# Transposing the row of maxima one group later in an attention and feed-forward kernel, with other groups for the middle tile's maxima and six buffers for the sums of p

## The chip, the cores and the metric

The kernel runs on one core of a Trainium2 chip. The metric is the device time of one execution in microseconds (us); several executions are timed, and the median counts. The engines have separate instruction streams and wait for each other through semaphores: PE multiplies matrices (its weight loads are listed apart as PEld), DVE, ACT and POOL do elementwise work and reductions, and SP issues the transfers.

## The reference

Attention for 8 batches of 8 heads, 1152 positions of width 64, in which the queries are averaged in pairs (576 rows are left), and then a feed-forward layer over the 4608 rows:

```
q_pool = q.reshape(B, H, S // 2, 2, D).mean(axis=3)
scores = (1 / sqrt(D)) * (q_pool @ k^T)
attn   = exp(scores - max over keys);  attn /= (sum over keys + 1e-9)
x      = attn @ v                      # 4608 x 512 after regrouping
h      = x @ w_in                      # 512 -> 2048
out    = (h - tanh(h)) @ w_out         # 2048 -> 512
```

## The kernel before, in words

**Two stages.** The attention stage goes through 32 pairs of heads; the feed-forward stage follows and uses the attention's output from device memory. Numbers are split in a high and a low part (`hi`, `lo`), so that each product is three matmuls.

**A clock of units.** The attention stage is ordered by hand. A pair has 36 units. Every sixth unit begins a group of three key tiles for one half of the queries, so a pair has six groups, which begin at its units 0, 6, 12, 18, 24 and 30. On each even unit `scores` (L271) issues eight matmuls into a `ps_s` tile: `hi` by `hi`, `hi` by `lo`, `lo` by `hi`, and last `ones_k` by `mb`, which subtracts the row's maximum. ACT then takes the exponential into the group's tile `p_f`. When a group is through, POOL adds its three key tiles' exponentials (`z_part`, L288, two additions into a tile `z`); 11 units after the group's begin `pv` (L294) multiplies `p_f` by v into `ps_o`. Once for each half of the queries, one group after that half's last `pv`, at units 11 and 29, `z_sums` (L314) multiplies its three `z` tiles by ones, into the single tile `ps_z`; until then those tiles are held. Each engine's queue holds its instructions in the order in which this loop issues them.

**Maxima.** The maxima of a pair must be known before its first scores. So, during the pair ahead of it, `max_part` (L224) multiplies `hi` by `hi` for three thirds of the keys and for five tiles of queries: tiles 0 to 3 into a `ps_s` tile, two in each group; the middle tile, 4, into `ps_z`. DVE reduces each into `mx` a unit later. `ps_s` has three buffers and is shared by scores and maxima; `ps_z` has one buffer, shared by the middle tile's maxima, the sums and the transposition.

**The row of maxima.** `max_rows` (L240) runs 23 units ahead of the pair (`row`, L436): on DVE two reductions into `nm`, then the two instructions that write `m2` (shown as `m` in the profile): a copy that rounds and a subtraction. Then, as many units after `row` as `steps` says, `turn` transposes `m2` on PE into `ps_z`, with ACT's copy to `mt` a unit later (`out`), `there` sends `mt` to `m_dram`, and `back` fetches it as two rows into `mb`. On SP's queue `back` waits until `there` has landed.

**What the change touches.** The pool `zp` that holds the tiles `z` (L147), `steps` (L436) and the list `mids` of the middle tile's three units (L438, and L451 for the third pair). The second pair's own `row, steps` (L449) and the first's (L443) stand apart: in the first pair everything is packed closer, and the maxima of the second and the third pair are taken there and in the second pair.

The order of the feed-forward stage is left to a scheduler.

Of the kernel before, what the change touches and what calls it, by code (L numbers as in the profile page):

```python
# [43 lines left out]
def kernel(  # L44
# [97 lines left out]
    with ExitStack() as actx:  # L142
# [1 line left out]
        sm = actx.enter_context(tc.tile_pool(name="sm", bufs=2))  # L144
        op = actx.enter_context(tc.tile_pool(name="op", bufs=1))
        pf = actx.enter_context(tc.tile_pool(name="pf", bufs=4))
        zp = actx.enter_context(tc.tile_pool(name="zp", bufs=4))  # L147
        vp = actx.enter_context(tc.tile_pool(name="vp", bufs=2))
        hl = actx.enter_context(tc.tile_pool(name="hl", bufs=3))
        ld = actx.enter_context(tc.tile_pool(name="ld", bufs=2))  # L150
# [29 lines left out]
        def add(u, f, *args, at=at):  # L180
            at.setdefault(u, []).append(lambda: f(*args))
# [251 lines left out]
        for pi in range(n_pair):  # L433
            u = pi * U
            units = dict(load=-92, query_sums=-80, hi_q=-70, hi_k=-68, hi_k2=-66, lo_q=-64, lo_k=-52, lo_k2=-46, load_v=-40)
            row, steps = -23, (4, 6, 12)  # L436
            spots = [x for g in range(6) for x in ((at, -60 + G * g + 5), (early, -60 + G * g + 6))]
            mids = [-49, -37, -31]  # L438
            if pi == 0:
                units.update(load=-60, query_sums=-52, hi_q=-51, hi_k=-50, hi_k2=-49, lo_q=-22, lo_k=-21, lo_k2=-20)  # L440
                spots = [(at, -48 + 2 * i) for i in range(12)]
                mids = [-43, -35, -27]
                row, steps = -24, (2, 3, 4)  # L443
            if pi < 3:
                v0 = -U * pi
                if pi == 1:
                    units.update(load=v0 - 58, query_sums=v0 - 25, hi_q=v0 - 20, hi_k=v0 - 19, hi_k2=v0 - 18, lo_q=-28, lo_k=-16, lo_k2=-10)
                    mids = [v0 + 5, v0 + 11, v0 + 17]
                    row, steps = v0 + 25, (2, 3, 6)  # L449
                if pi == 2:  # L450
                    mids = [v0 + 29, v0 + 35, v0 + 41]  # L451
                if pi > 0:
                    spots = [x for g in range(4) for x in ((early, v0 + 24 * (pi - 1) + G * g), (at, v0 + 24 * (pi - 1) + G * g + 2),
                                                           (at, v0 + 24 * (pi - 1) + G * g + 5))]
            add(u + units["load"], load, pi)
            add(u + units["query_sums"], query_sums, pi, dve if pi < 1 else pool)
            for what, f in (("hi", hi_part), ("lo", lo_part)):
                add(u + units[what + "_q"], f, pi, 0, SQ)
                add(u + units[what + "_k"], f, pi, SQ, 2 * SQ)
                add(u + units[what + "_k2"], f, pi, 2 * SQ, KQ)  # L460
            add(u + units["hi_k2"], middle, pi)
            for i, (when, x) in enumerate(spots):
                add(u + x, max_part, u + x, pi, *divmod(i, 3), at=when)
            for c, x in enumerate(mids):
                add(u + x, max_part, u + x, pi, 4, c)
            add(u + units["load_v"], load_v, pi)
            add(u + row, max_rows, u + row, pi, steps)
# [162 lines left out]
```

## Time and profile before

| | |
|---|---|
| median of 3 runs | 1810.62 us (1803.29 to 1811.96) |
| profiled execution, own time | 1805.21 us |
| its span | 1803.4 us |
| attention stage, about | 0 to 979 us of the span |
| one steady pair (480.00 to 509.21 us) | 29.21 us |
| PE, DVE, ACT, POOL busy in the span | 95%, 81%, 58%, 58% |
| mean granted TensorE clock | 0.991 |

In the profile's rows, an instruction is named by its engine, its line and by what it writes and reads (`mx<-ps_s`). Nearly all of the attention stage stands under L37, the line of the helper that records instructions in program order; tiles' names tell them apart. A number in brackets is the idle time of the engine before the instruction, with the instruction or transfer that ended it. In a timeline the first number is the start, the second the duration of the row from its first to its last instruction. Work is named here by the unit of the pair at which it is issued.

### The profile page before, as it was taken

The numbers are of one execution on the slowest core, as the hardware profiler recorded it, in microseconds if no ns is written. First come the engines' busy times: TensorE is split into PE (matmuls) and PEld (weight loads), VectorE is DVE, ScalarE is ACT, GpSimd is POOL, SyncE is SP. The second block draws the span as 40 slices with busy tenths as digits, with TensorE's granted clock in tenths as the row PEclk, the third lists the DMA queues.
The fourth block names the chain that finished last, engine by engine and source line by source line (L and its number), as shares of the span: only waits on it lengthen the run. The fifth ranks groups of instructions, "written<-read, shape, count | busy, mean of one in ns | idle before, by whom it ended". The sixth has DMA issues, their size and how long they took to land.

```text
span 1803.4 us, 31496 instructions
## 1 busy us (share of the span) xinstructions
PE 1705.4 (95%) x12224; PEld 1238.7 (69%) x12224; DVE 1454.6 (81%) x1854; ACT 1049.1 (58%) x1961; POOL 1038.6 (58%) x760
## 2 busy tenths in 40 slices
PE   6999999999999999999999999999999999999998
PEld 4656565656565656565666877878787878788886
DVE  6778777777787777787755999988888899888897
ACT  3455555555555555555545656665666566666676
POOL 3777676777676868677766373444444444333432
PEclk9999999999999999999999999999999999999999
DMA  3242424242424242424351721010101010100000
GB/s 142 85 140 73 140 71 142 71 141 72 141 72 141 71 142 71 142 78 134 90 193 63 291 66 52 20 51 19 52 19 52 18 54 20 43 15 33 30 21 14
DMA packets 73493, 148.09 MB, mean 82 GB/s; under 512 B 12032, under 2 KB 37248, under 8 KB 73344
## 3 DMA queue, kind: packets, MB, share of 16 engines
q1 hardware_dynamic: 73344, 146.10, 24.7%
q8 instruction: 95, 1.56, 0.4%
q14 instruction: 54, 0.44, 0.1%
HBM read 109.64 MB, written 36.42 MB: 81 GB/s over the span
## 4 chain that ended last, share of the span: by engine, by line
PE 71%; DVE 17%; DMA 4%; ACT 4%; POOL 3%; issue 2%; SPq 1%; DVEq 0%; POOLq 0%; ACTq 0%
PE ps_s L37 20%; PE ps_o L37 16%; PE ps_h L525 14%; PE ps_o L550 14%; PE ps_z L37 6%; DVE m L37 4%; DVE mx L37 3%; DVE g_s L541 2%; DVE g_w L539 1%; DVE g_s L540 1%; DMA x_f<-x_dram 1%; DMA x_r<-r_dram 1%; DVE g_w L538 1%; POOL g_lo L543 1%; DVE lo L37 1%
## 5 line engine op out<-in xcount | busy, mean ns | idle before, releaser
L37 DVE TENSOR_REDUCE mx<-ps_s 128x2 f32<-128x768 f32 x384 | 364.9, 953 | 211.0 <-PE ps_s L37 209.6
L37 ACT ACTIVATE p_f<-ps_s 128x576 f32<-128x576 f32 x576 | 352.6, 649 | 249.9 <-PE ps_s L37 227.8
L543 POOL TENSOR_TENSOR g_lo<-g_s,g_hi 128x512 fp32r<-128x512 f32 (+1 forms) x160 | 210.1, 1314 | 401.9 <-ACT g_hi L542 348.4
L37 POOL TENSOR_TENSOR z<-p_f 128x576 f32<-128x576 f32 x192 | 282.7, 1472 | 144.7 <-PE ps_z L37 129.1
L37 PE MATMUL ps_s<-hi 64*128 64x288 f32 (+1 forms) x1920 | 316.8, 358 | 19.0 <-ACT hi L37 8.6
L37 PE MATMUL ps_o<-p_f,v 128*64 128x288 f32 x2304 | 330.6, 423 | 2.6 <-ACT o_s L37 2.6
L525 PE MATMUL ps_h<-x,wi 128*128 128x512 f32 (+1 forms) x1320 | 295.8, 369 | 0.0
L37 POOL TENSOR_TENSOR z<-z,p_f 128x576 f32<-128x576 f32 x192 | 273.7, 1426 | 15.0
L37 PEld LDWEIGHTS ps_s<-hi 64*128 64x128 f32 x1920 | 170.5, 189 | 152.4 <-issue 73.3
L525 PEld LDWEIGHTS ps_h<-x,wi 128*128 128x128 f32 x1320 | 233.6, 188 | 47.4
L550 PE MATMUL ps_o<-wo,g_hi 128*128 128x512 f32 x936 | 255.8, 392 | 4.8 <-ACT g_hi L542 4.6
L37 PEld LDWEIGHTS ps_o<-p_f,v 128*64 128x64 f32 x2304 | 151.0, 139 | 115.3 <-issue 36.5
L550 PEld LDWEIGHTS ps_o<-wo,g_hi 128*128 128x128 f32 x936 | 173.4, 188 | 43.5 <-ACT g_hi L542 7.3
L542 ACT ACTIVATE g_hi<-g_s 128x512 fp32r<-128x512 f32 (+1 forms) x160 | 94.3, 589 | 142.9 <-DVE g_s L541 140.2
L37 PE MATMUL ps_s<-mb,ones_k 64*128 64x288 f32 x1152 | 171.9, 293 | 3.3 <-DMA mb<-m_dram 3.3
L37 PE MATMUL ps_s<-lo,hi 64*128 64x288 f32 x1152 | 172.9, 295 | 0.0
L37 PE MATMUL ps_s<-hi,lo 64*128 64x288 f32 x1152 | 172.3, 294 | 0.0
L538 DVE SCALAR_TENSOR_TENSOR g_w<-g_w,g_u 128x512 f32<-128x512 f32 (+1 forms) x160 | 171.1, 1069 | 0.0
L531 ACT ACTIVATE g_u<-ps_h 128x512 f32<-128x512 f32 (+1 forms) x160 | 87.7, 548 | 136.4 <-PE ps_h L525 136.1
L541 DVE COPY_PREDICATED g_s<-g_m,g_t 128x512 f32<-128x512 int32 (+1 forms) x160 | 139.3, 870 | 15.1 <-DVE g_s L540 0.5
L536 DVE SCALAR_TENSOR_TENSOR g_w<-g_u,ps_h 128x512 f32<-128x512 f32 (+1 forms) x160 | 100.3, 627 | 61.1 <-ACT g_t L532 39.4
L550 PE MATMUL ps_o<-wo,g_lo 128*128 128x512 f32 x468 | 148.0, 391 | 1.5 <-POOL g_lo L543 1.3
(73 smaller groups left out, 2647.4 us busy)
## 6 DMA issues: line engine op xcount, KB each, us to landing
q_n<-in_q_dram SPq DMA_DIRECT2D x32, 576.0 KB
kq<-in_k_dram SPq DMA_DIRECT2D x32, 576.0 KB
v<-in_v_dram SPq DMA_DIRECT2D x32, 576.0 KB
x_dram<-o_s SPq DMA_DIRECT2D x32, 288.0 KB
out_dram<-o_s SPq DMA_DIRECT2D x34, 256.0 KB
w_raw<-in_moe_w_in_dram SPq DMA_DIRECT2D x16, 512.0 KB
wi_dram<-w_hl SPq DMA_DIRECT2D x16, 512.0 KB
w_raw<-in_moe_w_out_dram SPq DMA_DIRECT2D x16, 512.0 KB
```

The source lines that it names most:

```text
L37: ins = self.tc.keep_in_program_order(f(*args, **kwargs))
L525: nc.tensor.matmul(h, wi[fc][:, w, c], x[:, c, 0:n], start=(j == 0), stop=(j == len(mm) - 1))
L531: nc.scalar.activation(u, h, AF.Square)
L536: nc.vector.scalar_tensor_tensor(w, u, -P0, h, op0=ALU.add, op1=ALU.mult)
L538: nc.vector.scalar_tensor_tensor(w, w, PL, u, op0=ALU.mult, op1=ALU.mult)
L539: nc.vector.scalar_tensor_tensor(w, s2, P2, w, op0=ALU.add, op1=ALU.mult)
L540: nc.vector.scalar_tensor_tensor(s1, s1, P1, w, op0=ALU.add, op1=ALU.mult)
L541: last = nc.vector.copy_predicated(s1, m.bitcast(I32), th).ins
L542: nc.scalar.activation(g_h, s1, AF.Copy)
L543: nc.gpsimd.tensor_tensor(g_l, s1, g_h.bitcast(F32), op=ALU.subtract)
L550: nc.tensor.matmul(po[j], g[:, ts], wo[fc][:, w], start=(fc == 0 and i == 0), stop=(fc == NF - 1 and i == 2))
```

## The change

The pool of `z` tiles grows from four to six buffers. In the usual pairs (the third and later) `turn` goes from 4 to 10 units after `row`, which is from unit 17 to unit 23 of the pair ahead; `out` goes along; `there` goes from 6 to 12 units after `row` and `back` from 12 to 16. The middle tile's first third changes places with it: it goes from unit 23 to unit 17. For the third pair, whose maxima are taken in the first pair, it goes from unit 29 to unit 27 of that first pair.

```diff
-        zp = actx.enter_context(tc.tile_pool(name="zp", bufs=4))
+        zp = actx.enter_context(tc.tile_pool(name="zp", bufs=6))
...
-            row, steps = -23, (4, 6, 12)
+            row, steps = -23, (10, 12, 16)
             spots = [x for g in range(6) for x in ((at, -60 + G * g + 5), (early, -60 + G * g + 6))]
-            mids = [-49, -37, -31]
+            mids = [-55, -37, -31]
...
                 if pi == 2:
-                    mids = [v0 + 29, v0 + 35, v0 + 41]
+                    mids = [v0 + 27, v0 + 35, v0 + 41]
```

PE's queue in a steady pair shows the exchange. `ps_z<-ident_r,m` is the transposition, `ps_z<-hi,bd` the middle tile's maxima, `ps_o<-p_f,v` the product with v. Before, ahead of the group of unit 18:

```order
L37 MATMUL ps_s<-mb_125,ones_k 128x288 x2
L37 MATMUL ps_s<-hi 128x384 x2
L37 MATMUL ps_z<-ident_r,m_787 20x128
L37 MATMUL ps_o<-p_f,v 64x288 x6
L37 MATMUL ps_s<-hi 128x384 x2
```

In the changed kernel, at the same place:

```order
L37 MATMUL ps_s<-mb_125,ones_k 128x288 x2
L37 MATMUL ps_s<-hi 128x384 x2
L37 MATMUL ps_z<-hi,bd_128 128x384
L37 MATMUL ps_o<-p_f,v 64x288 x6
L37 MATMUL ps_s<-hi 128x384 x2
```

The transposition has left this place; it now stands one group further on, where the middle tile's matmul was.

POOL's queue around the second group of a steady pair, with the engines whose semaphores each instruction waits for. `z<-p_f` is the first addition of a group, `z<-z,p_f` the second. Before:

```order
L37 TENSOR_TENSOR z<-p_f 128x576 [waits Activation_49]
L37 TENSOR_TENSOR z<-z,p_f 128x576 [waits Activation_49,Pool_49]
L37 TENSOR_TENSOR z<-p_f 128x576 [waits PE_49,Activation_49]
L37 TENSOR_TENSOR z<-z,p_f 128x576 [waits Activation_49,Pool_49]
L37 TENSOR_TENSOR z<-p_f 128x576 [waits Activation_49]
```

In the changed kernel, at the same place:

```order
L37 TENSOR_TENSOR z<-p_f 128x576 [waits Activation_49]
L37 TENSOR_TENSOR z<-z,p_f 128x576 [waits Activation_49,Pool_49]
L37 TENSOR_TENSOR z<-p_f 128x576 [waits Activation_49]
L37 TENSOR_TENSOR z<-z,p_f 128x576 [waits Activation_49,Pool_49]
L37 TENSOR_TENSOR z<-p_f 128x576 [waits Activation_49]
```

The wait for PE, which is the wait until an older `z` tile has been read, is gone from the middle addition; the order of POOL's instructions in the attention stage is the same.

DVE's queue in the first pair, from the row of the second pair's maxima on. Before:

```order
L37 TENSOR_TENSOR m_516<-nm,m_516 128x10
L37 TENSOR_TENSOR lo<-kq,hi 128x576 x2
L37 TENSOR_REDUCE mx<-ps_s 128x2 x2
L37 TENSOR_REDUCE mx<-ps_z 128x1
L37 TENSOR_SCALAR w_554<-w_554 128x512
```

In the changed kernel:

```order
L37 TENSOR_TENSOR m_516<-nm,m_516 128x10
L37 TENSOR_TENSOR lo<-kq,hi 128x576 x2
L37 TENSOR_REDUCE mx<-ps_s 128x2
L37 TENSOR_REDUCE mx<-ps_z 128x1
L37 TENSOR_REDUCE mx<-ps_s 128x2
```

The middle tile's reduction stands one place earlier. On PE its matmul now stands right ahead of the second pair's transposition, where it stood behind the maxima of unit 29; both use the single `ps_z`.

## The prediction

> **What bounds the kernel now.** I read the page's engines first, then the chain of waits by engine.
>
> ```profile
> PE 1705.4 (95%) x12224; PEld 1238.7 (69%) x12224; DVE 1454.6 (81%) x1854; ACT 1049.1 (58%) x1961; POOL 1038.6 (58%) x760
> PE 71%; DVE 17%; DMA 4%; ACT 4%; POOL 3%; issue 2%; SPq 1%; DVEq 0%; POOLq 0%; ACTq 0%
> ```
>
> PE is the bound, so what shortens the kernel is what PE waits for. The waits of PE alone, over the span and then over the steady part of the attention stage (60 to 975 us), name it; the columns are us in total, times, longest.
>
> ```profile
> PE ps_z L37 <- DVE m L37: 51.6, 31, 2.7
> ...
> PE ps_z L37 <- DVE m L37: 47.7, 29, 1.9
> PE ps_s L37 <- DVE mx L37: 6.6, 8, 1.2
> ```
>
> Almost all of PE's waiting there is for one thing: the transposition into `ps_z` waits for DVE's `m`, 47.7 / 29 = 1.645 us each time. Two more, 3.9 us, lie in the first pair. The timelines of one steady pair say why. First PE:
>
> ```profile
> 490.50 0.34 PE L37 MATMUL ps_s<-hi 64*128 64x384 f32 x2
> 492.46 0.23 PE L37 MATMUL ps_z<-ident_r,m 128*20 128x128 f32 x1 [1.63 <-DVE m L37]
> 492.62 1.68 PE L37 MATMUL ps_o<-p_f,v 128*64 128x288 f32 x12
> 494.23 0.58 PE L37 MATMUL ps_s<-hi 64*128 64x384 f32 x4
> 496.37 0.34 PE L37 MATMUL ps_s<-hi 64*128 64x384 f32 x2
> 496.64 0.45 PE L37 MATMUL ps_z<-hi,bd 128*128 128x384 f32 x1
> 497.01 1.68 PE L37 MATMUL ps_o<-p_f,v 128*64 128x288 f32 x12
> 498.62 0.58 PE L37 MATMUL ps_s<-hi 64*128 64x384 f32 x4
> 500.12 0.40 PE L37 MATMUL ps_s<-hi 64*128 64x288 f32 x2
> 500.75 0.34 PE L37 MATMUL ps_s<-hi 64*128 64x384 f32 x2
> ```
>
> From the maxima of unit 17 (490.50) to those of unit 23 (496.37) are 5.87 us; the next group, which has the middle tile instead of the transposition, takes 500.75 - 496.37 = 4.38. DVE, then POOL, at the same time:
>
> ```profile
> 488.85 0.96 DVE L37 TENSOR_REDUCE mx<-ps_s 128x2 f32<-128x768 f32 x1 [2.11 <-PE ps_s L37]
> 490.12 0.93 DVE L37 CAST m<-nm 128x10 fp32r<-128x10 f32 x1
> 491.09 1.32 DVE L37 TENSOR_TENSOR m<-nm,m 128x10 fp32r<-128x10 f32 x1
> 492.33 0.95 DVE L37 TENSOR_REDUCE mx<-ps_s 128x2 f32<-128x768 f32 x1
> ...
> 488.11 1.42 POOL L37 TENSOR_TENSOR z<-p_f 128x576 f32<-128x576 f32 x1 [3.33 <-PE ps_z L37]
> 489.61 1.42 POOL L37 TENSOR_TENSOR z<-z,p_f 128x576 f32<-128x576 f32 x1
> 490.99 1.39 POOL L37 TENSOR_TENSOR z<-p_f 128x576 f32<-128x576 f32 x1
> ```
>
> The two `m` instructions handle ten numbers a lane, yet take 0.93 and 1.32 us: the first ends at 491.05, where POOL's addition ends (491.03), the second at 492.41, where the next one ends (492.38). POOL's additions stand there because the first had waited 3.33 us for a `z` tile that `z_sums` still held. The second pair shows the chain without this:
>
> ```profile
> 69.69 0.17 DVE L37 CAST m<-nm 128x10 fp32r<-128x10 f32 x1
> 69.90 0.17 DVE L37 TENSOR_TENSOR m<-nm,m 128x10 fp32r<-128x10 f32 x1
> ...
> 70.76 1.42 POOL L37 TENSOR_TENSOR z<-p_f 128x576 f32<-128x576 f32 x1 [5.45 <-PE ps_z L37]
> ...
> 73.28 0.23 PE L37 MATMUL ps_z<-ident_r,m 128*20 128x128 f32 x1
> ```
>
> POOL was idle, each took 0.17 us, and that transposition, alone of the 30 after the first pair, did not wait.
>
> The Trainium skill, page "SBUF — State Buffer", section "Who interferes with whom", says that GpSimd and a VectorE instruction with two SBUF inputs, or a copy in a two-port mode, exclude each other for a whole instruction, and that a reduction never contends. By that rule the trace agrees: 0.17 us against 0.93 and 1.32, while the reductions keep 0.95.
>
> **The change part by part.**
>
> *The transposition a group later.* It reaches PE about 4.4 us later than now, and the chain is 1.63 us late now: the wait goes in either case. Its one PE instruction, ACT's copy, one transfer out and two in per pair are moved, none added. Exchanging it with the middle tile leaves PE's work the same over the two groups. Gain: 29 x 1.645 = 47.7 us; the wait of the first pair's own row stays. Nothing is late next on PE if DVE keeps up, which the next part decides.
>
> *The middle tile at unit 17* puts one more reduction on DVE between the `m` chain and the reduction of unit 18, and that one is tight everywhere:
>
> ```profile
> 499.10 0.96 DVE L37 TENSOR_REDUCE mx<-ps_s 128x2 f32<-128x768 f32 x1 [0.83 <-PE ps_s L37]
> ...
> 482.80 0.54 DVE L37 TENSOR_REDUCE mx<-ps_z 128x1 f32<-128x384 f32 x1
> ```
>
> It begins 0.48 us after its matmul (498.62), ends at 500.06, and the group's third scores start at 500.12, since they take its `ps_s` buffer. So every delay of it is a delay of PE. In the change's PE time, the group of unit 18 begins at 490.50 + (498.62 - 496.37) = 492.75, and its reduction wants DVE at 493.23. If the chain still ended at 492.41, DVE would reduce unit 17 from 492.33, the middle tile from 493.20 (0.87 later, as these follow each other), and unit 18 from 493.68: 0.45 us late, 29 x 0.45 = 13 us given back. If the chain is short, it is over by 490.5, unit 17 is reduced from about 490.95 to 491.9, the middle tile to 492.4, and nothing is late. So this edit costs 0 to 13 us, and the third decides.
>
> *Six `z` tiles.* POOL's first addition for the group of unit 6 needs that group's second exponential, the other additions the third:
>
> ```profile
> 485.99 1.19 ACT L37 ACTIVATE p_f<-ps_s 128x576 f32<-128x576 f32 x2
> 489.44 1.92 ACT L37 ACTIVATE p_f<-ps_s 128x576 f32<-128x576 f32 x3 [0.54 <-PE ps_s L37]
> ```
>
> Half of the first row is over at about 486.65, so POOL adds from there to about 489.6 instead of 488.11 to 491.03. The next group's additions need its second exponential, about 490.7. Between 489.6 and 490.7 POOL is idle, and the two `m` instructions, due at 490.12 and by 490.33, fall there: slack of 0.5 us ahead, 0.4 behind. I take 0 for the middle tile's cost. Additions after that stay where they are, being bound by exponentials.
>
> *The row's way back.* `there` and `back` are two groups from the first scores now, not three. In SP's queue of the steady pairs both still stand ahead of the load of v, which waits for a product of the next pair.
>
> ```profile
> 493.02 0.62 SPq L37 DMA_DIRECT2D m_dram<-mt  x1
> 494.96 0.56 SPq L37 DMA_DIRECT2D mb<-m_dram  x2
> ...
> 22.87 0.56 SPq L37 DMA_DIRECT2D mb<-m_dram  x2
> ...
> 26.84 0.76 PE L37 MATMUL ps_s<-mb,ones_k 64*128 64x288 f32 x2 [3.26 <-DMA mb<-m_dram]
> ...
> 508.78 0.29 PE L37 MATMUL ps_s<-mb,ones_k 64*128 64x288 f32 x2
> ```
>
> From the transposition to the second transfer's issue 2.5 us, and from issue to use, where PE waited for it, 3.97: about 6.5, say 7. In the change the transposition stands at 490.50 + 4.38 + 0.27 = 495.15, `mb` is there at about 502.2, and wanted at 508.78 - 1.63 = 507.15. Slack 5 us, cost 0.
>
> *The third pair's middle tile*, now right ahead of the first pair's transposition in the single `ps_z`:
>
> ```profile
> 49.39 0.23 PE L37 MATMUL ps_z<-ident_r,m 128*20 128x128 f32 x1 [1.21 <-DVE m L37]
> ...
> 49.26 1.42 DVE L37 TENSOR_TENSOR lo<-kq,hi 128x576 fp32r<-128x576 f32 x2
> 50.59 1.81 DVE L37 TENSOR_REDUCE mx<-ps_s 128x2 f32<-128x768 f32 x2
> ```
>
> The transposition must wait for the middle tile's reduction, behind both `lo` and one of those two reductions: 50.59 + 0.87 + 0.54, about 52.1 instead of 49.39. That costs 2.7 us once, between 0 (if other work there shortens) and 5 (if the longer idle slows the following matmuls).
>
> The skill's page "TensorE: Matmul & The Clock Gate", section "What's actually happening", has the clock halved after an idle window of some 3.4 us; one more such window at half speed would add an estimated 1.7 us here.
>
> *The last pair.* There `there` and `back` fall among large loads for the feed-forward stage, and the second of these now stands behind `back`. PE waits once near there already:
>
> ```profile
> 958.13 3.11 PE L37 MATMUL ps_o<-p_f,v 128*64 128x288 f32 x12 [2.55 <-ACT o_s L37]
> ```
>
> That wait hangs on those loads by way of DVE and ACT, so part of the last 1.9 us gained can go into it: 0 to 2, I take 1. The feed-forward stage's instructions are the same, reordered in its first tokens alone: 0, plus or minus 2.
>
> **Sum:** 1805.2 - 47.7 + 2.7 + 1.0 = 1761.2 us on the profiled execution's own time. That execution stands 5.4 below the median; the four known times average 1807.8, 2.6 above it. I add 2: **1763 us**.
>
> **The rivals.**
>
> *Shorter gain, 1776 us.* POOL still catches the `m` chain (slack 0.4 us), the middle tile's reduction pushes that of unit 18 back, and PE waits 0.45 us a pair: 13 us. For it: additions set free may collide with other DVE work as well. Against: all places where a reduction of that kind waits for PE have slack of at least 0.4 us.
>
> *No change, 1805 to 1811.* DVE becomes the bound and the 47.7 us return as waits for maxima. One steady pair by busy time:
>
> ```profile
> 480.00:509.21 29.21, 27.57 (x272) 17.84 (x272) 22.78 (x28) 16.05 (x31) 21.84 (x15) 1.00 0.34 109
> ```
>
> After the span and its length come PE, PEld, DVE, ACT, POOL. DVE's 22.78 us fit in 27.6, with 2 of them being the blocked chain. Against it, clearly; also here: the wait may simply have another cause than the order shows.
>
> *Slower, 1850.* `mb` arrives late at every pair's first scores. It decides from a round trip above 12 us, and eats the gain above 13.6; at 15 us it costs 29 x 3 = 87 us, 1763 + 87. For it: the 4.5 KB follow loads of 576 KB in one queue. Against: the slack of 5 us, and `there` now comes later after those loads.
>
> **How the numbers follow.** Forecast 0.73, shorter gain 0.14, no change 0.07, slower 0.04; 0.02 lies between. The range: 1753 (fastest run less 47.7, and 2 for the feed-forward order) to 1782 (shorter gain, 5 for the first pair and runs above the average). About 0.5% is what a measurement of this kernel tells from no change. Faster 0.89, same 0.06, slower 0.05.
>
> **What would show it.** PE's wait for `m` falls to about one, in the first pair and longer than 2.7 us; a steady pair takes 27.6 us; the `m` instructions take 0.17 us; POOL's waits for `ps_z` are gone; the third scores of the group of unit 18 follow without a wait. I am wrong if PE waits for `mb`, or if waits for `mx` grow to tens of us.

## The result

| | before | changed |
|---|---|---|
| median of the runs shown with the result | 1809.75 us (4 runs, 1803.29 to 1811.96) | 1740.66 us (4 runs, 1739.11 to 1741.33) |
| profiled execution's span | 1803.4 us | 1739.5 us |
| mean granted TensorE clock in it | 0.991 | 0.999 |

The ratio is 0.9623, with a 95% interval of 0.9597 to 0.9648. The change is faster, as forecast, but by 69 us between the medians instead of 48, and the time lies below the range of 1753 to 1782. Two things stand out beside the time: the changed kernel's runs lie within 2.2 us of each other where those of before spread over 8.7, and the granted clock has risen.

### The profile after

The page's engines, and then the waits of PE alone over the span (us in total, times, longest):

```profile
PE 1692.5 (97%) x12224; PEld 1231.8 (71%) x12224; DVE 1406.3 (81%) x1854; ACT 1047.0 (60%) x1961; POOL 1046.6 (60%) x760
```

```profile
PE ps_s L37 <- DMA mb<-m_dram: 4.5, 2, 3.4
PE ps_z L37 <- DVE mx L37: 3.5, 1, 3.5
PE ps_z L37 <- DVE m L37: 2.7, 1, 2.7
PE ps_s L37 <- ACT p_f L37: 1.7, 2, 0.9
PE ps_s L37 <- DVE mx L37: 1.6, 4, 0.6
```

The wait for `m`, 51.6 us before, is down to the first pair's own 2.7. The timelines of one steady pair, PE, DVE and POOL, answer to those that the prediction shows:

```profile
460.71 0.34 PE L37 MATMUL ps_s<-hi 64*128 64x384 f32 x2
460.98 0.44 PE L37 MATMUL ps_z<-hi,bd 128*128 128x384 f32 x1
...
462.96 0.57 PE L37 MATMUL ps_s<-hi 64*128 64x384 f32 x4
...
465.09 0.34 PE L37 MATMUL ps_s<-hi 64*128 64x384 f32 x2
465.36 0.23 PE L37 MATMUL ps_z<-ident_r,m 128*20 128x128 f32 x1
...
460.34 0.17 DVE L37 CAST m<-nm 128x10 fp32r<-128x10 f32 x1
460.55 0.17 DVE L37 TENSOR_TENSOR m<-nm,m 128x10 fp32r<-128x10 f32 x1
461.10 0.96 DVE L37 TENSOR_REDUCE mx<-ps_s 128x2 f32<-128x768 f32 x1 [0.38 <-PE ps_s L37]
461.97 0.55 DVE L37 TENSOR_REDUCE mx<-ps_z 128x1 f32<-128x384 f32 x1
463.44 0.96 DVE L37 TENSOR_REDUCE mx<-ps_s 128x2 f32<-128x768 f32 x1 [0.93 <-PE ps_s L37]
...
458.43 1.42 POOL L37 TENSOR_TENSOR z<-z,p_f 128x576 f32<-128x576 f32 x1
460.92 1.41 POOL L37 TENSOR_TENSOR z<-p_f 128x576 f32<-128x576 f32 x1 [1.08 <-ACT p_f L37]
```

POOL's second addition ends at 459.85 and its next begins at 460.92, when the exponentials are there; the two `m` instructions, at 460.34 and 460.55, fall into the gap and take 0.17 us each. `m` is ready 4.6 us ahead of the transposition, and the reduction of unit 18 (463.44) has 0.93 us in hand. The five rows of PE also show the group of unit 17 to 23: 465.09 - 460.71 = 4.38 us, where it took 5.87.

### Where the 63.9 us between the two spans went

The times at which the sums of a pair reach PE mark its length. A steady pair went from 29.21 to 27.50 us. Two kinds of pairs were longer than that before. In seven pairs the reciprocals of a batch made DVE late, and PE waited for a reduction: 0.87 us in six of them, 1.16 us in one. In six others PE ran at half clock behind the transposition. These rows are one of the latter, PE's timeline and then its time in windows (after the length come PE, PEld, DVE, ACT and POOL busy, the granted clock and the share of the transfers):

```profile
251.05 0.27 PE L37 MATMUL ps_z<-ident_r,m 128*20 128x128 f32 x1 [1.63 <-DVE m L37]
251.25 3.15 PE L37 MATMUL ps_o<-p_f,v 128*64 128x288 f32 x12
```

```profile
220.00:221.00 1.00, 0.78 (x5) 0.47 (x7) 1.00 (x2) 0.27 (x1) 0.92 (x2) 0.69 1.00 385
221.00:222.00 1.00, 1.00 (x8) 0.51 (x6) 0.04 (x1) 0.00 (x0) 0.62 (x1) 0.50 0.81 327
222.00:223.00 1.00, 1.00 (x8) 0.35 (x4) 0.00 (x0) 0.00 (x0) 0.00 (x0) 0.50 0.16 56
223.00:224.00 1.00, 1.00 (x8) 0.54 (x6) 0.00 (x0) 0.00 (x0) 0.00 (x0) 0.60 0.08 28
...
930.00:970.00 40.00, 35.54 (x347) 23.33 (x345) 19.77 (x19) 20.15 (x38) 29.34 (x20) 0.91 0.50 164
```

The twelve matmuls with v take 3.15 us there and 1.68 otherwise. The first four windows are such a stretch in another pair: a clock of 0.50 for (1 - 0.69) / 0.5 = 0.6 us of the first, for all of the next two, and for (1 - 0.60) / 0.5 = 0.8 us of the fourth, 3.4 us together. The last is the end of the attention stage, at 0.91. After the change, the stage from the first sums to the last is at full clock:

```profile
56.36:912.24 855.88, 853.28 (x8335) 553.76 (x8333) 634.48 (x829) 492.91 (x926) 684.39 (x465) 1.00 0.36 118
```

The account, in us of the two profiled spans:

| | forecast | measured |
|---|---|---|
| wait of the transposition, steady pairs: 28 x (29.21 - 27.50) | -47.7 (29 pairs) | -47.9 |
| stretches at half clock in those pairs | none | -8.9 |
| waits behind the reciprocals, 6 x 0.87 and 1.16 | none | -6.4 |
| last two pairs, their own transposition's 1.9 among it | +1.0, and 1.6 in the first row | -5.9 |
| first pair | +2.7 | +2.5 |
| feed-forward stage (825.0 to 827.3) | 0, plus or minus 2 | +2.3 |
| other pairs, small | none | +0.5 |
| sum | -44.0 | -63.8 |

### The profile page after: what moved, and what is told of

It reads as the page before. It is cut to its first block, busy times and chain, and to the rows that moved or that the text cites. A ratio compares the mean times of both kernels' runs of the same rounds, so it can differ in the third digit from the quotient of the medians.

```text
span 1739.5 us, 31429 instructions
## 1 busy us (share of the span) xinstructions
PE 1692.5 (97%) x12224; PEld 1231.8 (71%) x12224; DVE 1406.3 (81%) x1854; ACT 1047.0 (60%) x1961; POOL 1046.6 (60%) x760
## 4 chain that ended last, share of the span: by engine, by line
PE 76%; DVE 13%; ACT 4%; DMA 4%; issue 1%; POOL 1%; SPq 0%; DVEq 0%; POOLq 0%; ACTq 0%
PE ps_s L37 25%; PE ps_o L37 17%; PE ps_h L525 14%; PE ps_o L550 14%; PE ps_z L37 6%; DVE g_s L541 2%; DVE g_s L540 2%; DVE g_w L539 2%; DVE g_w L538 2%; DVE g_t L537 1%; DVE mx L37 1%; DVE g_w L536 1%; DMA x_r<-r_dram 1%; DMA out_dram<-o_s 1%; POOL g_lo L543 1%
## 5 line engine op out<-in xcount | busy, mean ns | idle before, releaser
L37 POOL TENSOR_TENSOR z<-p_f 128x576 f32<-128x576 f32 x192 | 292.4, 1523 | 107.8 <-ACT p_f L37 107.8
L37 PE MATMUL ps_o<-p_f,v 128*64 128x288 f32 x2304 | 323.0, 416 | 0.0
L37 POOL TENSOR_TENSOR z<-z,p_f 128x576 f32<-128x576 f32 x192 | 286.5, 1492 | 15.5 <-ACT p_f L37 0.5
L538 DVE SCALAR_TENSOR_TENSOR g_w<-g_w,g_u 128x512 f32<-128x512 f32 (+1 forms) x160 | 179.1, 1120 | 0.0
```

Source lines behind the costliest of these rows:

```text
L37: ins = self.tc.keep_in_program_order(f(*args, **kwargs))
L538: nc.vector.scalar_tensor_tensor(w, w, PL, u, op0=ALU.mult, op1=ALU.mult)
```

## The experiments

Each was timed beside the kernel before on the same chip; there were three chips, on which the kernel before had medians of 1805.32, 1807.24 and 1805.87 us. The runs of the first group asked which of the edits does what; those of the second, where the half clock comes from; the last pair of runs compares the change with a version of it.

### Six tiles alone

```diff
-        zp = actx.enter_context(tc.tile_pool(name="zp", bufs=4))
+        zp = actx.enter_context(tc.tile_pool(name="zp", bufs=6))
```

> The kernel before with six z tiles and nothing else. Theory: the m instructions were late only because POOL's additions, held up by a missing z tile, stood in their way. Then they take 0.17 us each, the transposition no longer waits where it always stood, a steady pair takes about 27.5 us, and the stretches at half clock go; the 0.87 us that seven pairs lose to the reciprocals stay (6 us), the 2.7 us that the change lost in the first pair do not arise: about 1744 us. Rival: only the move of the transposition removes the wait; then the m instructions stay at 0.93 and 1.32 us, PE's wait for m stays near 48 us, and the time is about 1800 to 1810 us.

Measured: 1738.11 us median (1737.81 to 1738.44), ratio 0.9632 (0.9592 to 0.9672). The transposition stands where it always stood, and does not wait. DVE, PE and POOL in one steady pair:

```profile
485.03 0.17 DVE L37 CAST m<-nm 128x10 fp32r<-128x10 f32 x1
485.24 0.17 DVE L37 TENSOR_TENSOR m<-nm,m 128x10 fp32r<-128x10 f32 x1
...
485.68 0.23 PE L37 MATMUL ps_z<-ident_r,m 128*20 128x128 f32 x1
...
483.12 1.42 POOL L37 TENSOR_TENSOR z<-z,p_f 128x576 f32<-128x576 f32 x1
485.62 1.41 POOL L37 TENSOR_TENSOR z<-p_f 128x576 f32<-128x576 f32 x1 [1.09 <-ACT p_f L37]
```

`m` is there at 485.41, 0.27 us ahead of the transposition. So the wait came from the missing `z` tile, by way of POOL and DVE, and the first rival is out. A steady pair takes 27.50 us, as in the change. The time is 6 us below my expectation; 3 of them are the reciprocals' pairs, which lose 0.42 us each here, not 0.87.

### The move alone

```diff
-        zp = actx.enter_context(tc.tile_pool(name="zp", bufs=6))
+        zp = actx.enter_context(tc.tile_pool(name="zp", bufs=4))
```

(against the changed kernel)

> The change without the two more z tiles. Theory: the transposition does not wait, since it comes 4.4 us later, but m still takes 0.93 and 1.32 us, the middle tile's reduction pushes that of unit 18 back, and PE waits there 0.45 us in each of 29 pairs: 13 us more than the change, about 1754 us. Rival: the move alone does all and the z tiles nothing: 1741 us. Second rival: the move alone does nothing: about 1800 us.

Measured: 1755.38 us median (1752.63 to 1756.24), ratio 0.9725 (0.9683 to 0.9766). DVE, then PE, in one steady pair:

```profile
496.36 0.93 DVE L37 CAST m<-nm 128x10 fp32r<-128x10 f32 x1
497.33 1.33 DVE L37 TENSOR_TENSOR m<-nm,m 128x10 fp32r<-128x10 f32 x1
498.58 0.95 DVE L37 TENSOR_REDUCE mx<-ps_s 128x2 f32<-128x768 f32 x1
499.45 0.54 DVE L37 TENSOR_REDUCE mx<-ps_z 128x1 f32<-128x384 f32 x1
499.92 0.94 DVE L37 TENSOR_REDUCE mx<-ps_s 128x2 f32<-128x768 f32 x1
...
500.92 0.40 PE L37 MATMUL ps_s<-hi 64*128 64x288 f32 x2 [0.44 <-DVE mx L37]
```

This is the price that the prediction worked out for the case that the chain stays late: the three reductions follow each other without a gap, and the third scores wait 0.44 us. A steady pair takes 27.95 us, 0.45 more than in the change. Either edit alone removes the long wait; the tiles alone leave nothing behind in a usual pair, the move alone leaves 0.45 us.

### Five tiles

```diff
-        zp = actx.enter_context(tc.tile_pool(name="zp", bufs=6))
+        zp = actx.enter_context(tc.tile_pool(name="zp", bufs=5))
```

(against the changed kernel)

> The change with five z tiles. Theory: only the second group of a half lacked a tile, and one more is enough: m at 0.17 us, the same time as the change, 1741 us. Rival: a second one is needed as well, m is late again and PE waits about 0.45 us a pair: 1754 us.

Measured: 1741.71 us median (1738.88 to 1743.83), ratio 0.9646 (0.9597 to 0.9695). `m` takes 0.17 us in the median again, and the change's 1740.66 lies in the spread. With the move in place, one more tile than before is enough; five tiles in the old order were not run.

### The third pair's middle tile where it was

```diff
-                    mids = [v0 + 27, v0 + 35, v0 + 41]
+                    mids = [v0 + 29, v0 + 35, v0 + 41]
```

(against the changed kernel)

> The change with the third pair's middle tile back at unit 29 of the first pair. Theory: PE's wait of 3.5 us for mx in the first pair falls to about 1 us; 2.5 us less than the change, about 1738 us. Rival: the sums, which then come right behind the middle tile in the same psum tile, wait instead, or half clock follows either way: 1740 to 1741 us.

Measured: 1736.72 us median (1736.01 to 1737.36), ratio 0.9624 (0.9584 to 0.9664). First the place in the changed kernel (PE), then in this one:

```profile
52.23 0.23 PE L37 MATMUL ps_z<-ident_r,m 128*20 128x128 f32 x1 [3.51 <-DVE mx L37]
...
53.29 3.14 PE L37 MATMUL ps_o<-p_f,v 128*64 128x288 f32 x12
```

```profile
48.83 0.23 PE L37 MATMUL ps_z<-ident_r,m 128*20 128x128 f32 x1 [1.21 <-DVE m L37]
...
50.28 1.68 PE L37 MATMUL ps_o<-p_f,v 128*64 128x288 f32 x12
52.46 1.16 PE L37 MATMUL ps_z<-z,ones 128*32 128x288 f32 x12 [0.51 <-DVE mx L37]
```

The wait is down from 3.51 to 1.21 us, and a stretch at half clock that the change has there is gone (3.14 against 1.68 us for the matmuls with v); the sums now wait 0.51 instead. That the stretch came with the longer wait is likely and not shown: the kernel before, with a wait of 1.21 us there, has one in its profile as well (49.72 to 53.13 us). The sums start at 52.46 us here and at 56.36 in the changed kernel's profile, 3.9 us for both together.

### An idle time of PE put back by another way

The kernel before with six tiles, and reductions on DVE ahead of the subtraction that writes `m`, from the fourth pair on:

```diff
+            if pi > 2:
+                for _ in range(2):
+                    dve.tensor_reduce(w.mx[:, 8, 0:1], w.hi[:, 0:768].bitcast(F32), axis=AX.X, op=ALU.max)
             dve.tensor_tensor(m2[:, 1], nm, m2[:, 0].bitcast(F32), op=ALU.subtract)
```

> Six z tiles, the transposition at its old place, and from the fourth pair on two added reductions on DVE ahead of the subtraction that writes m, which change no result (they write a column of mx that has been read). They make m late by about 1.75 us without any z tile lacking: PE waits about 1.5 us in each of 29 pairs, 29 x 1.5 = 44 us over the 1738 us of the six tiles alone: 1782 us. Theory: the stretches at half clock come from such idle times of PE; then some of them return, the mean clock falls below 0.998 in part of the runs and these runs take 5 to 15 us more, 1785 to 1797 us, spread by several us. Rival: they came from something else in the kernel before (POOL held up, transfers); then the clock stays at 0.999 to 1.0, and all runs lie within 1 to 2 us at about 1782.

Measured: 1787.15 us median (1784.50 to 1789.70), ratio 0.9882 (0.9848 to 0.9916). The waits of PE for `m` from 60 to 975 us, and one of them:

```profile
PE ps_z L37 <- DVE m L37: 42.0, 29, 1.7
...
480.94 0.23 PE L37 MATMUL ps_z<-ident_r,m 128*20 128x128 f32 x1 [1.43 <-DVE m L37]
```

In the profiled execution no steady pair shows a half clock; its two stretches lie in the first pair (from 49.95 us) and in the feed-forward stage (from 1169.52 us). Across the four runs, time follows clock: 1784.50 us at 0.999, 1787.02 and 1787.27 at 0.998, 1789.70 at 0.996; where the stretches of the other three lie, no trace shows. So the expected return of the half clock did not come: the time at full clock explains nearly all, and by itself this run settles nothing between theory and rival.

### A longer idle time

```diff
-                for _ in range(2):
+                for _ in range(3):
```

> As the run with two added reductions, but with three: PE waits about 2.7 us in each of 29 pairs and DVE is late for the reduction of unit 18 as well; 78 us and more over 1738, about 1820 us at full clock. Theory: the longer the idle time, the more often the clock is halved behind it: then most pairs show a stretch at half clock, each costs 1.7 us, the mean clock falls to 0.98 or below, and the time is 1840 us or more. Rival: the stretches are as rare as in the kernel before (a clock of 0.99) or absent (0.999): 1820 to 1828 us.

Measured: 1874.57 us median (1867.43 to 1878.11), ratio 1.0361 (1.0312 to 1.041), clock 0.962 to 0.969. Waits from 60 to 975 us, PE in one pair, and a window behind that transposition:

```profile
PE ps_z L37 <- DVE m L37: 76.7, 27, 3.1
```

```profile
488.32 0.28 PE L37 MATMUL ps_z<-ident_r,m 128*20 128x128 f32 x1 [2.84 <-DVE m L37]
488.53 3.15 PE L37 MATMUL ps_o<-p_f,v 128*64 128x288 f32 x12
```

```profile
488.50:491.50 3.00, 3.00 (x13) 1.23 (x12) 0.64 (x1) 0.27 (x1) 0.00 (x0) 0.50 0.07 26
```

26 of the 28 steady pairs have a length of 31.5 us or more, the other two 30.4 and 30.8: the half clock follows nearly every idle time of 2.8 us. It followed 6 in 28 at 1.6 us (1.9 in one of the six), and none in the profile at 1.43. The rival, that the half clock has nothing to do with this idle time, is out: here no `z` tile is missing and POOL is not held, and it is back in nearly every pair.

### An idle time between the two

```diff
-                    dve.tensor_reduce(w.mx[:, 8, 0:1], w.hi[:, 0:768].bitcast(F32), axis=AX.X, op=ALU.max)
+                    dve.tensor_reduce(w.mx[:, 8, 0:1], w.hi[:, 0:1056].bitcast(F32), axis=AX.X, op=ALU.max)
```

(against the run with two added reductions)

> As the run with two added reductions, each over 1056 numbers instead of 768, about 0.3 us longer each: PE waits about 2.0 us in each of 29 pairs, between the 1.63 us of the kernel before (6 stretches at half clock in 29 pairs) and the 2.84 us of three reductions (nearly all pairs). At full clock that is 1738 + 29 x 2.0 = 1796 us and a little for the reduction of unit 18. Theory: the share of pairs with a stretch at half clock grows with the idle time; here it lies between 6 and 27 of 29, about 10 to 15, which costs 17 to 25 us: 1813 to 1825 us, clock 0.98 to 0.99. Rival: the share does not depend on the length, only on how the pairs fall in time: then 6 or fewer, or nearly all; under 1808 or over 1840 us.

Measured: 1873.48 us median (1867.86 to 1878.11), ratio 1.0379 (1.0352 to 1.0406). The run did not do what it was for. DVE, POOL and PE in one pair:

```profile
480.93 2.53 DVE L37 TENSOR_REDUCE mx<-hi 128x1 f32<-128x1056 f32 x2
483.38 0.96 DVE L37 TENSOR_TENSOR m<-nm,m 128x10 fp32r<-128x10 f32 x1
...
482.92 1.40 POOL L37 TENSOR_TENSOR z<-z,p_f 128x576 f32<-128x576 f32 x1
...
484.39 0.28 PE L37 MATMUL ps_z<-ident_r,m 128*20 128x128 f32 x1 [2.83 <-DVE m L37]
```

The subtraction came at 483.38, found POOL's addition at work since 482.92 and ended with it (482.92 + 1.40 = 484.32, the subtraction at 484.34). So PE waited 2.83 us, the same as with three reductions, and the time is the same; 23 of 28 steady pairs were hit here. It says nothing of an idle time of 2.0 us. It shows once more what made `m` late before.

Where the half clock begins can be read from the clock records in the traces of the kernel before and of the three runs with added reductions. The stretches of one trace begin on a grid: those in the steady pairs of the kernel before at 220.38, 251.10, 312.54, 343.26, 462.73 and 582.20 us, which is 9, 18, 9, 35 and 35 times 3.413 us apart, and each lasts one interval of this grid (in the runs with a wait of 2.83 us also two). So I added up PE's idle time in each interval that ran at full clock, over the steady pairs of the four traces. All 52 intervals with 1.64 us or more were followed by half clock, none with 1.61 us or less was, and 3 of the 11 at 1.62 or 1.63 us were.

A wait of 1.43 us cannot reach that; the waits of 1.6 us of the kernel before stand just at it, if they fall into one interval whole; and one of 2.83 us misses it only where the grid cuts it near its middle, which is so in all 7 of the 56 pairs that were spared. So length and position both count. The first pair and the feed-forward stage do not keep to this border: 1.28 us were enough in the first pair of the kernel before, and 1.80 us in the feed-forward stage of the changed kernel's second profile were not. Why is open.

### The change and its version side by side

The last two kernels are the changed one, and the one with the third pair's middle tile at unit 29, on one chip.

> The changed kernel beside the next one on one chip: 1740.7 us again, within 1 us, since without idle times behind m no stretch at half clock is left but one in the first pair.

> The change with the third pair's middle tile at unit 29 of the first pair, as before, beside the change itself: 2.5 to 5 us less than it, 1736 to 1738 us. Rival: the difference seen was that of the chips; then both are equal within 1 us.

Measured: the change 1741.24 us median (1740.65 to 1741.89), ratio 0.9639 (0.9624 to 0.9653); the version 1736.44 (1735.50 to 1736.54), ratio 0.9611 (0.9596 to 0.9625). No run of the version is as slow as the fastest of the change: 4.8 us less. In the two profiles 3.2 us of it lie ahead of the first sums (56.49 against 53.25 us), 0.9 in the feed-forward stage, whose order the scheduler makes anew. It is the fastest of the kernels tried. The changed kernel's four runs here had clocks of 0.996 to 0.999 and lie within 1.3 us, 1741.50 us at 0.996 and 1740.65 at 0.999: a lower mean clock did not cost time there, so not every stretch at half clock is paid for.

## Why the prediction was right and wrong

**Right: the cause and its size.** The transposition's wait, the additions of POOL that stand in DVE's way, the missing `z` tile behind them: the six tiles alone confirm each link. The term 29 x 1.645 = 47.7 us measured 47.9 in 28 steady pairs, and the last pair's on top. The reading that six tiles let the chain fall between two additions, with slack of 0.5 us ahead and 0.4 behind, measured 0.49 (459.85 to 460.34) and 0.20 (460.72, the end of `m`, to 460.92). Had it failed, the price of 0.45 us a pair, which the rival of the shorter gain rested on, was right too: the move alone shows it to the hundredth.

**Right: the first pair.** A wait of 3.51 us for `mx`, 2.5 us lost before the second pair, against 2.7; a stretch at half clock lies there in both profiles. The two versions side by side, of which one has no such stretch, put the price at 3.2 us, half clock included, within the 0 to 5 that was given.

**Wrong: the step "Gain: 29 x 1.645 = 47.7 us" as the whole gain.** It counted the idle time and nothing that followed from it. The clock was looked at closely where the first pair waits, not in the steady pairs: the one whose rows the prediction shows ran at 1.00, and over the stage the mean was this:

```profile
60.00:975.00 915.00, 856.86 (x8252) 554.55 (x8252) 686.63 (x826) 492.48 (x921) 667.17 (x461) 0.99 0.34 110
```

Of 915 us a mean of 0.99 is some 9 us, and it is the term that was left out: 8.9 us in the steady pairs and part of what the last two gained. The idle time was followed by half speed for 3.4 us in six of 28 pairs, and each time cost about 1.5 us more, nearly as much as the wait.

The prediction weighed the Trainium skill's page "TensorE: Matmul & The Clock Gate", section "What's actually happening", in the first pair alone, for an idle window of about 3.4 us. The traces differ from that figure: here half clock came behind an idle time of 1.6 us in 6 of 28 pairs and behind 2.83 us in 49 of 56. What has about that length in them is the interval of the grid, 3.41 us.

**Wrong: "I add 2" for the spread of the runs.** I took the spread of the runs before for something that the changed kernel would share. It was in the main the same half clock. Of the 21 runs of the kernel before beside the experiments, eight ordered by clock: 1795.64, 1797.93 and 1799.45 us at 0.997, 1802.29 at 0.995, 1805.32 at 0.991, 1811.76 at 0.989, 1810.30 at 0.988, 1816.54 at 0.986. A stretch of 3.4 us at half speed lowers the mean by 0.5 x 3.4 / 1803 = 0.0009, and costs 1.5 us; from 0.997 to 0.988 are ten stretches, 15 us; 11 to 15 were measured. The clocks of the runs before that are shown with the result are not on record, so that they are dearer than the profiled one by half clock is inferred. Without these idle times the changed kernel has neither the cost nor the spread: the median's gain, 69.1 us, exceeds that of the spans, 63.9.

**Wrong: no term for the reciprocals, and the sign at the last pairs.** In the seven pairs with reciprocals PE waited for a reduction, 6.4 us in all. The rows, DVE of the kernel before and then of the changed one:

```profile
529.19 1.80 DVE L37 TENSOR_TENSOR lo<-kq,hi 128x576 fp32r<-128x576 f32 x1
530.92 1.41 DVE L37 SCALAR_TENSOR_TENSOR rec<-rec 128x36 f32<-128x36 f32 x1
```

```profile
496.00 0.75 DVE L37 TENSOR_TENSOR lo<-kq,hi 128x576 fp32r<-128x576 f32 x1
496.67 1.41 DVE L37 SCALAR_TENSOR_TENSOR rec<-rec 128x36 f32<-128x36 f32 x1
```

`lo` no longer stands behind an addition of POOL. The six tiles alone halve the loss (0.42) with `lo` still at 1.8 us, and the whole change ends it. The move alone ends it in five of the seven pairs, those in which `lo` takes 0.75 us; in the other two `lo` takes 2.02 us and PE waits 0.7 us. So it is the new order that frees `lo`. Which part of the order, no run shows. At the end of the stage PE does wait for `mb` in the last pair, 1.14 us, as feared:

```profile
888.46 0.58 PE L37 MATMUL ps_s<-mb,ones_k 64*128 64x288 f32 x2 [1.14 <-DMA mb<-m_dram]
```

But the wait of 2.55 us for `o_s` is gone there, and so are the two stretches at half clock in the 40 us at 0.91, which cost at most 0.09 x 40 = 3.6 us.

**The rivals.** No change and slower are out: `mb` is in time in all steady pairs, and DVE has room. The feed-forward stage's new order costs 2.3 us; PE's waits there rise from 17.0 to 19.1 us.

## What to carry to other kernels

Follow a wait back through the engines until something is missing, here buffers of a tile that only the sums hold; giving two of them was worth as much as the whole change, and the reordering alone left a part of the delay at another place. Count an idle time of PE with what follows it: read the granted clock in short windows right behind the wait, since a mean of 0.99 over a stage can hide a term of 10 us. Here a wait that was shorter by 0.2 us was free of that price. If the runs of a kernel spread more than their neighbours do, list their clocks beside their times before treating the spread as noise.

## What the runs showed of the hardware that was not expected

- Half speed of PE, for 3.4 us or twice that at a clock of 0.50, came behind idle times of 1.6 us in 6 of 28 steady pairs, of 2.83 us in 49 of 56, and of 1.43 us in none of the profiled execution.
- The stretches begin on a grid of 3.413 us. In the steady pairs of four traces they followed each of the 52 full-clock intervals of it with 1.64 us or more of idle time, and none with 1.61 us or less.
- The mean clock changes from run to run, and the time of the kernel before with it: 1795.6 to 1816.5 us at clocks of 0.997 to 0.986.
- An instruction on ten numbers a lane took 0.17 us with POOL idle and up to 1.33 us beside an addition on POOL, ending within 0.03 us of it.
